# The ELU of a half step's last tile behind the next half step's copy, two places for g and tanh, and weight sums and conversions at other hooks

## The chip, the core and the metric

One core of a Trainium2 chip runs the kernel. The metric is the device time of one launch in microseconds. The core has TensorE (PE, matrix products), VectorE (DVE), ScalarE (ACT), GpSimd (POOL) and SyncE (SP, which here only issues DMAs). Each engine takes its instructions in the order of its own queue, and a wait in front of an instruction holds all that stand behind it in that queue.

## What is computed

Three layers follow one another: a linear attention whose q and k go through a softmax, a mixture of four experts on its output, and a feed-forward layer with ELU. Inputs of the last layer's weights come as float64.

```python
def reference(q, k, v, domain_probs, w1, w2, w_in, w_out):
    q_s = softmax(q over head_dim); k_s = softmax(k over seq)
    kv = einsum('bhsd,bhse->bhde', k_s, v)
    x = einsum('bhsd,bhde->bhse', q_s, kv) -> (2304, 512)
    p = domain_probs / sum(domain_probs)
    x = sum over e of p[:, e] * (relu(x @ w1[e]) @ w2[e])   # w1 (4,512,1024)
    h = x @ w_in                                            # (512, 2048)
    return where(h > 0, h, exp(min(h, 0)) - 1) @ w_out      # (2048, 512)
```

## The kernel before

**Precision and products.** Every float32 operand of a matmul is split into a high part and a low part, and a product takes three matmuls (high by high, high by low, low by high). The first product of a block (tokens by hidden columns) is made from seven partial products of quarter blocks instead of eight, with sums and differences of quarters of the weights and of the tokens.

**Steps.** The first part of the run does the attention, and the first expert unit plainly beside it. From about 290 us on the work goes in 30 steps, numbered i, which are pairs (s, b): s = 0 to 9 is a group of hidden columns, b = 0 to 2 a third of the 2304 tokens. s = 0 to 5 belong to the experts (s below 5 in a form with a fast second product, `second_product`), s = 6 to 9, from about 842 us, to the ELU layer. A change of s comes every three steps.

**Half steps.** A step has two half steps, and each of them seven products p0 to p6 of six 128x384 matmuls (L1110), which go into four PSUM banks A, B, C, D; in the second half step A changes its part with C, and B with D. Behind p1, p3 and p5 stands a chunk each: twelve 128x512 matmuls (L1162 to L1164) of the second product of the step before. What the other engines do behind each product:

- p0: ACT copies C_ to a tile s5 (L1307).
- p1: ACT copies B_ to A_ (L1309). p2 writes into B_ again, so p2 waits for this copy.
- p2: DVE adds D_ = B_ + s5 (L1312). p4 writes into B_ again.
- p3: A_ is finished: ELU of A_.
- p4: DVE adds C_ = B_ + s5 (L1319).
- p5: D_ is finished: ELU of D_, and behind the chunk ELU of C_.
- p6: B_ is finished: ELU of B_, the half step's last tile, in the code right ahead of the next half step's p0.

**ELU of a tile** (`elu`): relu, exp and tanh on ACT (L1134 to L1136; m, e_ and t), e_ = (e_ + 1) t on DVE (L1137), then `flush()`, which issues the parts of the tile before (high part gh on ACT, L1144; low part gl on POOL, L1145), then g = max(h, 0) + e_ on DVE (L1140). The parts of g wait in a list until the next tile's flush. t and g have one place each (tags qh and ql), so a tile's g can be written only when the parts of the tile before have been made. e_ has one place too; it and s5 are two halves of one buffer, which the rows show as `extra`. In the rows a tile is named by the bank or the buffer it uses: m and h are PSUM banks or m tiles, and xh, xl, hpa and gx are buffers that take parts.

**What sets the order.** Side work is laid on numbered hooks: `at(t, fn)` in the attention part, `at2(i, k, fn)` in the steps, SH = 24 hooks in each step. A hook runs when PE's program reaches it, so a hook's number sets where in the queues of DVE, ACT, POOL and SP its instructions stand. `w1_steps` makes the high and low parts of four weight tiles for one s and half: hi(k) on ACT (L734), lo(k) on DVE (L744), and the differences `sums1` and `sums2` on DVE (L748 to L754); its dictionary gives the hook of each, with 13 more for the first half's, which stand in the last step of the s before. `convert` turns a 128x512 tile of float64 weights into float32: five DVE instructions (L455, L461, L465, L471, L474), an exp on ACT (L468) and a store in ACT's queue (L477); its load is issued on SP some hooks earlier. There are 32 such conversions. The evacuations of the second product are on DVE too (L1271 in the fast form, L1169 and L1175 in the chunks), those of s = 6 on ACT (L1173).

Of the kernel before, what the change touches and what calls it, by code (L numbers as in the profile page):

```python
# [21 lines left out]
def tile_attention_moe_moe(  # L22
# [692 lines left out]
    def w1_steps(s, p):  # L715

        r, t = [], []

        def begin():
            r.append(w1r.pop((s, p)).rearrange("p j (d f) -> p j d f", d=KD))  # L720
            for _ in range(4):
                t.append(wp.tile([P, 2, KD, P], F32R, tag="w1", name="w1s"))
            if s % 2:
                t[0], t[2] = t[2], t[0]
            hi(0)

        def src(k):
            return (r[0][:, 0], r[0][:, 1, 2:], r[0][:, 1], r[0][:, 0])[k]

        def dst(k, hl):  # L730
            return t[k][:, hl, :2] if k == 1 else t[k][:, hl]

        def hi(k):
            nc.scalar.activation(out=dst(k, 0), in_=src(k), func=AF.Copy)  # L734
            if k == 3:
                w1s[s, p] = dict(
                    A11=(t[0], 0), A12=(t[0], 2), A22=(t[1], 0),
                    S1=(t[2], 0), S2=(t[2], 2), S3=(t[3], 0), S4=(t[3], 2),
                )

        tt = nc.vector.tensor_tensor

        def lo(k):
            tt(out=dst(k, 1), in0=src(k), in1=dst(k, 0).bitcast(F32), op=ALU.subtract)  # L744

        def sums1():
            f1, f2 = r[0][:, 0], r[0][:, 1]
            tt(out=f1[:, :2], in0=f1[:, :2], in1=f2[:, :2], op=ALU.subtract)  # L748
            tt(out=f2[:, :2], in0=f2[:, :2], in1=f2[:, 2:], op=ALU.add)

        def sums2():
            f1, f2 = r[0][:, 0], r[0][:, 1]
            tt(out=f2[:, 2:], in0=f2[:, 2:], in1=f1[:, :2], op=ALU.subtract)
            tt(out=f1[:, 2:], in0=f1[:, 2:], in1=f2[:, 2:], op=ALU.subtract)  # L754

        m = int(s >= S_MOE)
        return {
            -5: begin, -4: lambda: lo(0), -2: sums1, 0: lambda: hi(1), 1: lambda: lo(1), 4: sums2,
            6 - m: lambda: hi(2), 7 - m: lambda: lo(2), 9 - m: lambda: hi(3), 11 - 2 * m: lambda: lo(3),
        }  # L760

    w2g = {}
# [68 lines left out]
    NCONV = 2 * F2 // P  # L831
    later = lambda n, fn: at2(0, n, fn)
    end1 = NB * S_FAST * SH
    CONV = [(at, t, 2, True) for t in (12, 30, 48, 122, 142, 160)]
    CONV += [(later, 34 + 26 * n, 3, False) for n in range(13)]
    CONV += [(later, end1 + 13 + 14 * n, 1, True) for n in range(3)]
    end2 = NB * S_MOE * SH
    CONV += [(later, end2 + 2 + 14 * n, 1, True) for n in range(NCONV - len(CONV))]
    for s, (put, t, d, aside) in enumerate(CONV):
        put(t - 8, lambda s=s, x=aside: convert_load(s, x))  # L840
        for n, fn in zip((0, 1, 2, 3, 5, 6, 8), convert(s, aside)):
            put(t + d * n, fn)
    for i, (s, b) in enumerate(STEPS):
        more = s + 1 < len(STEPS) // NB
        if b == 0:
# [7 lines left out]
        if b == 0:  # L853
# [11 lines left out]
            if s == S_MOE:  # L865
                a1, b1, a2, c2, b2, d2 = (42, 42, 72, 77, 82, 91)
            elif s == S_MOE + 1:
                a2, b2, c2, d2, a1, b1 = (21, 23, 29, 33, 38, 42)
            elif s == S_MOE + 2:
                a2, b2 = (14, 16)  # L870
            if s >= S_FAST:
                at2(i, a2, lambda s=s: w_load(s + 1, 0, 1))
                at2(i, b2, lambda s=s: w_load(s + 1, 1, 1))
# [246 lines left out]
            out=gl, in0=h, scalar=0.0, in1=gh.bitcast(F32), op0=ALU.max, op1=ALU.subtract  # L1120
        )

    waiting = []

    def flush():
        while waiting:
# [2 lines left out]
    def elu(i, h, f, half):  # L1129


        m = tmp.tile([P, TB], F32, tag="y", name="m")
        t = tmp.tile([P, TB], F32, tag="qh", name="t")
        nc.scalar.activation(out=m, in_=h, func=AF.Relu, scale=-1.0)  # L1134
        nc.scalar.activation(out=e_, in_=m, func=AF.Exp, scale=-1.0)  # L1135
        nc.scalar.activation(out=t, in_=m, func=AF.Tanh, scale=-0.5)  # L1136
        nc.vector.scalar_tensor_tensor(out=e_, in0=e_, scalar=1.0, in1=t, op0=ALU.add, op1=ALU.mult)  # L1137
        flush()
        g = tmp.tile([P, TB], F32, tag="ql", name="g")
        nc.vector.scalar_tensor_tensor(out=g, in0=h, scalar=0.0, in1=e_, op0=ALU.max, op1=ALU.add)  # L1140
        gh, gl = take(i, half, f)

        def parts():
            nc.scalar.activation(out=gh, in_=g, func=AF.Copy)  # L1144
            nc.gpsimd.tensor_tensor(out=gl, in0=g, in1=gh.bitcast(F32), op=ALU.subtract)  # L1145

        waiting.append(parts)
# [142 lines left out]
    for i, (s, b) in enumerate(STEPS):  # L1290
# [5 lines left out]
        for fp in range(2):  # L1296
# [5 lines left out]
            for p in range(len(PRODUCTS)):  # L1302
# [5 lines left out]
                elif p == 1:  # L1308
                    nc.scalar.activation(out=A_, in_=B_, func=AF.Copy)  # L1309
                    flush_late()  # L1310
                elif p == 2:
                    nc.vector.tensor_tensor(out=D_, in0=B_, in1=s5, op=ALU.add)  # L1312
                elif p == 3:
# [13 lines left out]
                elif p == 6:  # L1327
                    if idx in PLACES and fast(i - 1):
                        second_product(i - 1, PLACES.index(idx))
                    if fast(i):  # L1330
                        last = quarter_a12(i, fp, B_)
                        flush_late()
                        late.append(last)
                    else:
                        act(i, B_, f2, 0)
                if fp == 1:
                    if p == 0:
                        ring_load(len(OPS) * (i + 1))
# [10 lines left out]
                if p == 5 and not fast(i):  # L1349
                    if moe:  # L1350
                        relu(i, D_, f1, 1)
                    act(i, C_, f2, 1)
    flush()
    for c in CHUNKS:
        queue.append((len(STEPS) - 1, c))
# [54 lines left out]
```

## Time and profile before

| | before |
|---|---|
| median of 3 runs | 1293.41 us (1289.06 to 1294.11) |
| the profiled execution, its own time | 1294.12 us |
| its span in the profile | 1292.3 us |
| PE, matmul | 1209.5 us busy (94%) |
| PE, weight loads | 1110.5 us (86%) |
| DVE | 840.0 us (65%) |
| ACT | 631.8 us (49%) |
| POOL | 509.5 us (39%) |
| granted TensorE clock, mean | 0.98 of 2.4 GHz |

Busy shares are means over the run. An engine's idle time matters where another waits for it, so the views that count are the waits (per engine, which instruction waited, for whom, how long) and the timeline of single stretches. A row of the timeline may stand for several equal instructions (x2); the idle time and its releaser in brackets are those ahead of the first. Ends of matmuls are modelled: a 128x384 matmul reads 0.33 us, while the next one starts 0.17 us later.

### The profile page before, as it was taken

Reading aid. Unit: us, or ns where it says so; the run is one execution under the profiler, and the core shown is the slowest. Engines: PE = TensorE matmul, PEld = TensorE weight load, DVE = VectorE, ACT = ScalarE, POOL = GpSimd, SP = SyncE. Lnnn points to the kernel's source line nnn. Section 1 sums busy time; section 2 is a strip of 40 time slices with the busy share of each in tenths; the row PEclk is TensorE's granted clock in tenths of the full one; section 3 lists DMA queues with packets and bytes.
Section 4 is the critical chain, followed back from the end, with each engine's and each line's share of the span. In section 5 each row is a group of like instructions: output and inputs, shape, how many; then the busy total and the mean of one; then the engine's idle time right before and its main releaser. Section 6 shows DMA issues by size and latency. Waiting matters only on the chain.

```text
span 1292.3 us, 20568 instructions
## 1 busy us (share of the span) xinstructions
PE 1209.5 (94%) x7336; PEld 1110.5 (86%) x7336; DVE 840.0 (65%) x1486; ACT 631.8 (49%) x1361; POOL 509.5 (39%) x484
## 2 busy tenths in 40 slices
PE   7799999999999999999999999988888999999998
PEld 6588888888999999999999998877777878888887
DVE  6877787545676686776777765667465565456443
ACT  6444543235445454445554434546566445555442
POOL 4522552007446456455456423237223322322221
PEclk7899998999999999999999999999999999999999
DMA  8454565816656657657667578988757554644442
GB/s 223 138 150 147 191 206 209 284 57 225 241 195 241 230 181 268 225 190 268 224 214 257 191 281 267 336 276 273 285 187 269 177 204 170 215 166 154 167 165 82
DMA packets 155174, 272.32 MB, mean 211 GB/s; under 512 B 12864, under 2 KB 77888, under 8 KB 155072
## 3 DMA queue, kind: packets, MB, share of 16 engines
q1 hardware_dynamic: 145856, 254.23, 58.1%
q10 hardware_dynamic: 9216, 16.78, 3.5%
q8 instruction: 58, 0.95, 0.3%
q14 instruction: 44, 0.36, 0.1%
HBM read 224.83 MB, written 46.14 MB: 210 GB/s over the span
## 4 chain that ended last, share of the span: by engine, by line
PE 57%; DVE 18%; ACT 10%; issue 5%; POOL 5%; DMA 4%; SPq 0%; ACTq 0%; DVEq 0%; POOLq 0%
PE o L1249 14%; PE m L1110 11%; PE h L1110 10%; PE o L974 6%; PE h L974 6%; DVE g L1140 2%; ACT t L1136 2%; PE o L1164 2%; PE o L1163 2%; PE o L1162 2%; DVE accB L1271 1%; ACT extra L1135 1%; DVE w1s L744 1%; DMA r<-in_w_dram 1%; POOL xh L1145 1%
## 5 line engine op out<-in xcount | busy, mean ns | idle before, releaser
L1110 PE MATMUL m<-xh,w1s 128*128 128x384 f32 x840 | 251.1, 344 | 40.7 <-ACT h L1309 16.5
L1110 PE MATMUL h<-xh,w1s 128*128 128x384 f32 x840 | 247.0, 340 | 13.8 <-ACT m L1309 13.0
L1110 PEld LDWEIGHTS m<-xh,w1s 128*128 128x128 f32 x840 | 156.5, 191 | 53.1 <-ACT h L1309 21.1
L1110 PEld LDWEIGHTS h<-xh,w1s 128*128 128x128 f32 x840 | 156.1, 190 | 21.5 <-ACT m L1309 18.5
L1110 PE MATMUL m<-xl,w1s 128*128 128x384 f32 x420 | 142.6, 340 | 0.0
L1110 PE MATMUL h<-xl,w1s 128*128 128x384 f32 x420 | 141.8, 338 | 0.0
L1137 DVE SCALAR_TENSOR_TENSOR extra<-extra,t 128x384 f32<-128x384 f32 x96 | 58.5, 610 | 101.3 <-ACT t L1136 101.1
L974 PE MATMUL o<-w2t,hpa 128*128 128x512 f32 x432 | 120.2, 406 | 1.2 <-DVE hpa L1006 1.0
L974 PE MATMUL h<-xh,w1t 128*128 128x256 f32 (+1 forms) x512 | 114.1, 301 | 0.1
L974 PEld LDWEIGHTS h<-xh,w1t 128*128 128x128 f32 x512 | 88.0, 196 | 5.3 <-POOL w1t L421 0.4
L1249 PE MATMUL o<-w2g,xh 128*128 128x256 f32 x540 | 91.5, 284 | 0.0
L974 PEld LDWEIGHTS o<-w2t,hpa 128*128 128x128 f32 x432 | 77.0, 192 | 15.5 <-DVE hpa L1006 2.8
L1249 PE MATMUL o<-w2g,hpa 128*128 128x256 f32 x540 | 88.9, 282 | 0.0
L1249 PE MATMUL o<-w2g,xl 128*128 128x256 f32 x540 | 87.6, 283 | 0.0
L1135 ACT ACTIVATE extra<-m 128x384 f32<-128x384 f32 x96 | 50.4, 525 | 64.9 <-DVE g L1140 63.1
L1110 PEld LDWEIGHTS m<-xl,w1s 128*128 128x128 f32 x420 | 80.1, 191 | 1.2
L1110 PEld LDWEIGHTS h<-xl,w1s 128*128 128x128 f32 x420 | 79.8, 190 | 1.2
L1249 PEld LDWEIGHTS o<-w2g,xh 128*128 128x128 f32 x540 | 79.4, 193 | 0.0
L974 PE MATMUL h<-xl,w1t 128*128 128x256 f32 (+1 forms) x256 | 78.5, 307 | 0.0
L1249 PEld LDWEIGHTS o<-w2g,hpa 128*128 128x128 f32 x540 | 76.2, 190 | 0.0
L1249 PEld LDWEIGHTS o<-w2g,xl 128*128 128x128 f32 x540 | 76.1, 191 | 0.0
L775 POOL TENSOR_TENSOR w2g<-r,w2g 128x512 fp32r<-128x512 f32 x35 | 47.3, 1363 | 57.2 <-ACT w2g L774 57.2
(263 smaller groups left out, 2873.6 us busy)
## 6 DMA issues: line engine op xcount, KB each, us to landing
xh<-xs SPq DMA_DIRECT2D x210, 384.0 KB, 5.3
xl<-xs SPq DMA_DIRECT2D x210, 384.0 KB, 6.0
r<-in_w_dram SPq DMA_DIRECT2D x60, 256.0 KB, 4.0
xs<-stage SPq DMA_DIRECT2D x43, 256.0 KB, 3.6
xs<-xh SPq DMA_DIRECT2D x21, 384.0 KB, 4.4
xs<-xl SPq DMA_DIRECT2D x21, 384.0 KB, 4.3
r<-scratch ACTq DMA_DIRECT2D x28, 256.0 KB, 5.9
gt<-in_w_out_dram SPq DMA_DIRECT2D x10, 512.0 KB, 5.3
```

Source lines behind the costliest of these rows:

```text
L744: tt(out=dst(k, 1), in0=src(k), in1=dst(k, 0).bitcast(F32), op=ALU.subtract)
L775: nc.gpsimd.tensor_tensor(out=t[:, 1], in0=src, in1=t[:, 0].bitcast(F32), op=ALU.subtract)
L974: nc.tensor.matmul(out, lhsT, rhs, **kw)
L1110: nc.tensor.matmul(dst, t[:, wl, c + dl, :], x[xl_][:, dl, :], start=(n == 0 and p < 2), stop=(n == 5), skip_group_check=True,)
L1135: nc.scalar.activation(out=e_, in_=m, func=AF.Exp, scale=-1.0)
L1136: nc.scalar.activation(out=t, in_=m, func=AF.Tanh, scale=-0.5)
L1137: nc.vector.scalar_tensor_tensor(out=e_, in0=e_, scalar=1.0, in1=t, op0=ALU.add, op1=ALU.mult)
L1140: nc.vector.scalar_tensor_tensor(out=g, in0=h, scalar=0.0, in1=e_, op0=ALU.max, op1=ALU.add)
L1162: nc.tensor.matmul(o, gh, w[:, 0, :], start=(f == 0), stop=False)
L1163: nc.tensor.matmul(o, gh, w[:, 1, :], start=False, stop=False)
L1164: nc.tensor.matmul(o, gl, w[:, 0, :], start=False, stop=(f == FS - 1))
L1249: nc.tensor.matmul(o, l, r, start=(first_write and m == 0 and c != 1), stop=(m == 5), skip_group_check=True)
```

## The change

Five things are done. First, the ELU of B_ behind p6 is put in a list, `later_elu`, and taken from it behind the next half step's A_ copy (L1309 of before). Second, t and g get two places each, used in turn (`halves`). Third, in `w1_steps` the second high part goes from hook 0 to -1, its low part from 1 to 0, `sums2` from 4 to 1, the third high part from 6 (5 in the ELU layer) to 4, its low part from 7 (6) to 5, the fourth high part from 9 (8) to 8, and its low part from 11 (9) to 10 (9). Fourth, the conversions: in the attention part five instead of six, none of them at 122; in the fast steps 15 at a distance of 22 hooks instead of 13 at 26, and within one the pieces stand closer together; then three at 12 hooks' distance instead of 14; in the ELU steps nine instead of ten, the first 40 hooks into that layer instead of 2, so that step 18 has none. Fifth, one weight load (b2 for s = 8) moves from hook 16 to 18.

```diff
@@ w1_steps
-            -5: begin, -4: lambda: lo(0), -2: sums1, 0: lambda: hi(1), 1: lambda: lo(1), 4: sums2,
-            6 - m: lambda: hi(2), 7 - m: lambda: lo(2), 9 - m: lambda: hi(3), 11 - 2 * m: lambda: lo(3),
+            -5: begin, -4: lambda: lo(0), -2: sums1, -1: lambda: hi(1), 0: lambda: lo(1), 1: sums2,
+            4: lambda: hi(2), 5: lambda: lo(2), 8: lambda: hi(3), 10 - m: lambda: lo(3),
@@ conversions
-    CONV = [(at, t, 2, True) for t in (12, 30, 48, 122, 142, 160)]
-    CONV += [(later, 34 + 26 * n, 3, False) for n in range(13)]
-    CONV += [(later, end1 + 13 + 14 * n, 1, True) for n in range(3)]
+    CONV = [(at, t, 2, True) for t in (12, 30, 48, 146, 164)]
+    CONV += [(later, 34 + 22 * n, 2, False) for n in range(15)]
+    CONV += [(later, end1 + 13 + 12 * n, 1, True) for n in range(3)]
...
-    CONV += [(later, end2 + 2 + 14 * n, 1, True) for n in range(NCONV - len(CONV))]
+    CONV += [(later, end2 + 40 + 12 * n, 1, True) for n in range(NCONV - len(CONV))]
...
-        put(t - 8, lambda s=s, x=aside: convert_load(s, x))
-        for n, fn in zip((0, 1, 2, 3, 5, 6, 8), convert(s, aside)):
-            put(t + d * n, fn)
+        put(t - 7, lambda s=s, x=aside: convert_load(s, x))
+        for n, fn in zip((0, 1, 2, 3, 4, 5, 7) if d == 1 else (0, 2, 4, 6, 10, 12, 16), convert(s, aside)):
+            put(t + n, fn)
@@ elu
-        t = tmp.tile([P, TB], F32, tag="qh", name="t")
+        if not halves:
+            for tag in ("qh", "ql"):
+                halves[tag] = tmp.tile([P, 2 * TB], F32, tag=tag, name="half")
+        k = slice(turns[0] % 2 * TB, (turns[0] % 2 + 1) * TB)
+        turns[0] += 1
+        t, g = halves["qh"][:, k], halves["ql"][:, k]
...
-        g = tmp.tile([P, TB], F32, tag="ql", name="g")
@@ steps, behind p1
                     nc.scalar.activation(out=A_, in_=B_, func=AF.Copy)
                     flush_late()
+                    while later_elu:
+                        elu(*later_elu.pop(0))
@@ steps, behind p6
-                    else:
-                        act(i, B_, f2, 0)
+                    elif moe:
+                        relu(i, B_, f2, 0)
+                    else:
+                        later_elu.append((i, B_, f2, 0))
```

**ACT at a boundary of two half steps near the end.** L1307 and L1309 are the two copies of the new half step (L1312 and L1314 of after), the trio L1134 to L1136 (L1140 to L1142) is the ELU of a tile, L1144 (L1149) the high part. Before:

```order
L1134 ACTIVATE m_12065<-m_2883 128x384
L1135 ACTIVATE extra_2884<-m_12065 128x384
L1136 ACTIVATE t_12066<-m_12065 128x384
L1144 ACTIVATE xl_91<-g_12048 128x384
L1134 ACTIVATE m_12081<-m_2882 128x384
L1135 ACTIVATE extra_2884<-m_12081 128x384
L1136 ACTIVATE t_12082<-m_12081 128x384
L1144 ACTIVATE xh_90<-g_12073 128x384
L1307 ACTIVATE extra_2884<-h_2880 128x384
L1309 ACTIVATE m_2883<-h_2881 128x384
```

After:

```order
L1140 ACTIVATE m_11891<-m_2875 128x384
L1141 ACTIVATE extra_2876<-m_11891 128x384
L1142 ACTIVATE half_8692<-m_11891 128x384
L1149 ACTIVATE xl_91<-half_8693 128x384
L1312 ACTIVATE extra_2876<-h_2872 128x384
L1314 ACTIVATE m_2875<-h_2873 128x384
L1140 ACTIVATE m_11919<-m_2874 128x384
L1141 ACTIVATE extra_2876<-m_11919 128x384
L1142 ACTIVATE half_8692<-m_11919 128x384
L1149 ACTIVATE xh_90<-half_8693 128x384
```

The trio of the last tile and the high part that it flushes have moved from ahead of the two copies to behind them.

**DVE at a change of s in the fast steps.** L1271 (L1276 of after) are evacuations of the second product, L744 the low parts of the weights; `w1s_4492` is the one of the third tile that the next step's products read, L753 and L754 are `sums2`. Before:

```order
L455 TENSOR_SCALAR ce_97<-x64_4547 128x512
L1319 TENSOR_TENSOR h_2880<-h_2881,extra_2884 128x384
L1201 SCALAR_TENSOR_TENSOR xl_91<-h_2880,xl_91 128x384
L1206 SCALAR_TENSOR_TENSOR gt_96<-m_2882,gt_96 128x384 x2
L1215 TENSOR_TENSOR gt_96<-gt_96 128x384
L1271 SCALAR_TENSOR_TENSOR accB_93<-o_3110,pn_86,accB_93 128x256 x3
L744 TENSOR_TENSOR w1s_4492<-r_4232,w1s_4492 128x512
L744 TENSOR_TENSOR w1s_4655<-r_4279,w1s_4655 128x512
```

After (there the tile is `w1s_4493`):

```order
L753 TENSOR_TENSOR r_4230<-r_4230 128x256
L754 TENSOR_TENSOR r_4230<-r_4230 128x256
L1319 TENSOR_TENSOR m_2874<-h_2873,extra_2876 128x384
L1276 SCALAR_TENSOR_TENSOR accB_93<-o_3102,pn_86,accB_93 128x256 x3
L744 TENSOR_TENSOR w1s_4493<-r_4230,w1s_4493 128x512
L1326 TENSOR_TENSOR h_2872<-h_2873,extra_2876 128x384
L1206 SCALAR_TENSOR_TENSOR xl_91<-h_2872,xl_91 128x384
L1211 SCALAR_TENSOR_TENSOR gt_96<-m_2874,gt_96 128x384 x2
```

The low part now stands ahead of the C_ add (L1319, L1326 of after) and of what follows that add, one group of evacuations earlier; the next tile's L744 is no longer its neighbour.

**DVE in the attention part, at hook 122.** L1006 makes a part of the first expert unit, L238 and L240 are the sums that the attention's ek is made from.

```order
 L322 TENSOR_REDUCE qm<-accB 96x12
 L647 TENSOR_TENSOR sum<-sum,xl 128x2x384
-L455 TENSOR_SCALAR ce<-gt 128x512
 L1006 SCALAR_TENSOR_TENSOR hpa<-h,hpa 128x256
 L238 TENSOR_TENSOR ek<-m,ek 128x512
 L240 TENSOR_TENSOR ek<-m,ek 64x128
-L461 TENSOR_SCALAR gt<-gt 128x512
 L388 TENSOR_TENSOR xl<-m,xh 128x576
```

The conversion's first two instructions no longer stand there.

## Rows read from the trace of the kernel before

**Rows 1.** Waits of PE, 842 us to the end: total us, times, longest us.

```profile
PE m L1110 <- ACT h L1309: 14.9, 10, 4.1
PE h L1110 <- ACT m L1309: 12.6, 12, 2.4
PE m L1110 <- DVE m L1319: 5.0, 3, 2.9
PE m L1110 <- DVE g L1140: 1.6, 1, 1.6
PE o L1164 <- POOL xh L1145: 1.3, 2, 1.0
```

**Rows 2.** Waits of PE, 290 to 842 us.

```profile
PE m L1110 <- DVE w1s L744: 13.0, 5, 3.1
```

**Rows 3.** Waits of DVE, 842 us to the end.

```profile
DVE g L1140 <- POOL xh L1145: 23.8, 23, 2.4
```

**Rows 4.** Timeline of a half step: start, us, engine, line, operation [idle before, releaser].

```profile
1235.53 0.56 DVE L1140 SCALAR_TENSOR_TENSOR g<-m,extra 128x384 f32<-128x384 f32 x1 [0.95 <-POOL gx L1145]
1238.01 0.33 PE L1110 MATMUL m<-xh,w1s 128*128 128x384 f32 x1
1238.18 0.39 PE L1162 MATMUL o<-w2s,xh 128*128 128x512 f32 x1
...
1238.67 0.56 DVE L1140 SCALAR_TENSOR_TENSOR g<-h,extra 128x384 f32<-128x384 f32 x1 [0.95 <-POOL hpa L1145]
...
1240.95 0.48 ACT L1309 ACTIVATE h<-m 128x384 f32<-128x384 f32 x1
1241.48 0.44 PE L1110 MATMUL m<-xh,w1s 128*128 128x384 f32 x1 [0.38 <-ACT h L1309]
...
1242.89 0.57 DVE L1312 TENSOR_TENSOR h<-m,extra 128x384 f32<-128x384 f32 x1
...
1243.67 0.39 PE L1162 MATMUL o<-w2s,xh 128*128 128x512 f32 x1
...
1246.43 0.33 PE L1110 MATMUL m<-xh,w1s 128*128 128x384 f32 x1
```

**Rows 5.** Windows: us, busy PE, PEld, DVE, ACT, POOL, clock, DMA share, GB/s.

```profile
193.00:201.00 8.00, 5.46 (x32) 4.64 (x33) 6.72 (x16) 4.44 (x9) 2.22 (x2) 0.65 0.27 101
553.00:561.00 8.00, 8.00 (x46) 8.00 (x47) 6.75 (x12) 2.52 (x5) 1.86 (x2) 0.79 0.44 139
927.00:935.00 8.00, 7.81 (x40) 7.17 (x41) 4.00 (x7) 3.59 (x8) 1.47 (x2) 1.00 0.57 196
1000.00:1008.00 8.00, 6.43 (x19) 5.90 (x20) 2.24 (x4) 4.12 (x10) 1.17 (x2) 0.57 0.00 1
```

**Rows 6.** Timeline around the longest wait on L1309: ACT and PE.

```profile
995.29 0.60 ACT L1173 ACTIVATE accB<-o 128x512 f32<-128x512 f32 x1 [4.57 <-PE m L1110]
...
1001.57 0.69 PE L1110 MATMUL m<-xh,w1s 128*128 128x384 f32 x1 [4.12 <-ACT h L1309]
```

**Rows 7.** Timeline at the first change of s: DVE and PE.

```profile
364.21 2.10 DVE L744 TENSOR_TENSOR w1s<-r,w1s 128x512 fp32r<-128x512 f32 x2
...
364.94 0.62 PE L1110 MATMUL m<-xh,w1s 128*128 128x384 f32 x2 [2.33 <-DVE w1s L744]
```

**Rows 8.** Timeline in the attention part: DVE and PE.

```profile
190.44 3.45 DVE L455 TENSOR_SCALAR ce<-gt 128x512 uint16<-128x512 uint16 x1
...
195.54 0.70 PE L283 MATMUL m<-accB,ek 128*64 128x65 f32 x8 [3.46 <-ACT ek L244]
```

**Rows 9.** Timeline of DVE in step 18.

```profile
856.35 1.21 DVE L471 SCALAR_TENSOR_TENSOR ce<-gt,ce 128x512 uint16<-128x512 uint16 x1
```

**Rows 10.** Instructions of L1137 and L1140: ns minimum/median/maximum, first and last start.

```profile
L1137 DVE SCALAR_TENSOR_TENSOR extra<-extra,t x96: 541/559/1370, 850.6 to 1272.8; 128x384 f32<-128x384 f32 x96
...
L1140 DVE SCALAR_TENSOR_TENSOR g<-h,extra x48: 556/558/560, 851.7 to 1274.3; 128x384 f32<-128x384 f32 x48
```

More of the change, by code (lines that the diff above doesn't have):

```diff
@@ L869, in tile_attention_moe_moe @@
             elif s == S_MOE + 2:
-                a2, b2 = (14, 16)
+                a2, b2 = (14, 18)
             if s >= S_FAST:
@@ L1121, in relu @@
         )
-    waiting = []
+    waiting, later_elu = [], []
+    halves, turns = {}, [0]
     def flush():
@@ L1352, in tile_attention_moe_moe @@
                     act(i, C_, f2, 1)
+    while later_elu:
+        elu(*later_elu.pop(0))
     flush()
```

## The prediction, made before the change was run

> **What bounds the kernel now.** TensorE (PE) is busy nearly all the time, so a change that leaves its instructions and their order alone can only shorten the stretches in which it stands still or runs at half its clock. I read PE's waits by stage first. In the ELU stage (842 us to the end) two rows tell most of it: PE waits for ACT's copy A_<-B_ (L1309) for 14.9 and 12.6 us, over 22 of the 24 half steps [rows 1]. In the stage before, PE waits five times, 13.0 us in all, for DVE's weight parts (L744), once at each change of s [rows 2]. Then I asked what makes the copy late, with DVE's waits: g (L1140) waits for POOL's gl (L1145), 23.8 us in the largest of four such rows, one for each buffer that gl writes [rows 3]. The timeline of an undisturbed half step shows the chain [rows 4]: g(D) starts only when POOL is done (0.95 idle), C's tile follows, g(C) waits 0.95 again, the last tile B's ACT work follows that, and the copy of the next half step comes last, at 1240.95. PE was through with its chunk 0.38 before 1241.48, when it starts p2. p1, whose result the copy reads, was over at 1238.01 + 0.33 = 1238.34. So the copy was ready to run 2.6 us before it did.
>
> The third loss is the granted clock. It is at the upper level, 2.4 GHz, in most of the run, and in a few stretches PE drops to 1.2 GHz for a part of them, each time just behind a long wait: 8 us stretches at a mean of 0.65, 0.79 and 0.57 [rows 5]. Four read 0.79 (at 553, 865, 960 and 1056 us; one stands in the rows) and one 0.82 (at 361 us). One minus the mean, times 8, is what each lost at most: 2.8 + 4 x 1.7 + 1.4 + 3.4 = 14.4 us.
>
> **The change part by part. The last tile's ELU behind the copy, and two places for t and g.** These belong to one chain. Work it out on [rows 4]. g(D) at 1235.53 had stood 0.95 behind a free DVE. With a second place it needs no POOL and starts about 1234.6. exp(C) waits for g(D) alone, and one tile later g(C) runs at about 1236.8 to 1237.4 rather than 1238.67. B's relu, exp and tanh no longer stand ahead of the copy. The s5 copy goes when p0 is over, and the A copy when p1 is: 1238.34 plus its 0.48 is 1238.87, against 1241.43. It is 2.56 us earlier, and 2.2 us before PE runs dry (1241.48 - 0.38), so in the steady half step the wait goes wholly. Where a half step is disturbed, 2.56 us are there to take it up. The longest wait is 4.12 us [rows 6], and the nine others of its row come to 14.9 - 4.1 = 10.8, 1.2 each; so 4.12 - 2.56 = 1.6 us stay. That one comes from ACT's queue: its 4.57 idle before 995.29 lies behind a conversion's store (L477), which waits for DVE. Gain: 27.5 - 1.6 = 25.9 us. The first matmul behind a wait also takes 0.44 against 0.33 [rows 4]; 27 waits (22 here, 5 below) x 0.11 are 2.9 us more.
>
> What this adds: the parts of C now run behind the copy and behind B's relu, exp and tanh. Chunks read them, but from step 20 on none before p3's, which starts at 1243.67 [rows 4], and by the chain above they are done near 1241.8. In step 19 the first chunk reads them at once, and its wait on POOL (1.3 us in two [rows 1]) changes place rather than going: nothing taken, 1.3 either way. g(B) and e_(B) now stand ahead of the D_ add (L1312) in DVE's queue. The add ended at 1243.46, and p4, which overwrites what it reads, starts at 1246.43 [rows 4], so there are 3.0 us of room; g(B), by the chain above, is done near 1241.5, before the add ran in the old order. Nothing taken; the third rival prices the other case. At the end of the kernel the last ELUs stand in their old order: nothing.
>
> **Weight sums and parts at earlier hooks.** The wait at 364.94 shows the chain: two L744 of 1.05 each, started at 364.21, behind the evacuations of the second product, and PE waits 2.33 [rows 7]. In the new order the second L744 comes later, and the one that PE needs (lo2) stands one hook earlier. The last evacuation ahead of it is released by a matmul 38 before the need, not 8. Thirty matmuls of 384 columns at 0.17 apart (1238.01 to 1238.18 [rows 4]) are 5.1 us; with 256 columns, two thirds of that, 3.4. The longest of the five waits is 3.1 [rows 2]. All 13.0 go; the other end is 5 x (3.1 - 2.3) = 4 us that stay, if a stretched DVE instruction of a microsecond gets between.
>
> **Conversions at other hooks.** In the attention stage DVE's L455 at 190.44 took 3.45 us, and 3.46 us of PE's wait for ek follow it through L1006, L238 and ACT [rows 8]. In the new order no L455 stands there: -3.2, between 0 (some other long row in its place) and -3.46. In step 18 conversions are gone; L471 at 856.35 took 1.21 [rows 9] just ahead of the C_ add (L1319) for which PE waited 2.9 of the 5.0 us [rows 1]. Taken: -2.9, and -1.6 for the one wait on g (L1140), a bank that now frees a POOL wait sooner; between 0 and -6 together. What comes in their place: two conversions more in the stage before 842 us, at 22 hooks' spacing instead of 26, and two in each of the steps 20 to 23. Each is five DVE instructions; of the two whose rows stand here one took 1.21 and one 3.45 us [rows 8, 9]. Nearly all of it lies beside PE's work; for the pieces that come out I take +5, about two such conversions, between 0 and +18 (first rival).
>
> **Clock.** If the waits go, the lapses behind them should go too, but not every long wait had one (behind a wait at 927 us the clock read 1.00 [rows 5]), so the tie is loose, and smaller waits stay. I take two thirds of 14.4: -9.6, between 0 and -14.4.
>
> **Sum.** -25.9 - 2.9 - 13.0 - 3.2 - 4.5 + 5 - 9.6 = -54.1 us. The profiled run took 1294.12 for a span of 1292.3, 0.7 above the median of 1293.41, so 1240.0 stands against that run and the median alike. Everything at its best gives -25.9 - 1.6 - 2.9 - 13.0 - 3.46 - 6 - 14.4, or -67: 1227.
>
> **Rivals.** *First: half of it arrives.* The conversion's store sits in ACT's queue and holds ACT until DVE is through: 4.57 us at 995.29 [rows 6]. Conversions in the ELU stage now follow each other at 12 hooks, not 14. If each of the nine there costs ACT as much, 2.0 us over the room of 2.56 come out on PE: 18 us. With such waits the lapses of the clock stay, 9.6: 1240 + 27.6, about 1268. Against it: ten conversions ran in that stage, and the waits on L1309 show one of 4.1 us and the rest at 1.2 on average [rows 1].
>
> *Second: DVE and POOL get in each other's way.* So far g waits for POOL, so the two take turns. Freed of it, e_ (L1137) can run beside gl. Its median is 0.559 and its longest 1.370 us [rows 10]. Two on the path in a half step, 0.81 longer each, are 1.6 x 24 = 39 us: 1279. Against it: by the chain above gl(D) is issued behind C's tanh, so it runs beside g(C), not beside e_, and g, with one operand in PSUM, stayed within 556 to 560 ns in the 48 cases of one form [rows 10], and the other form reads alike. The Trainium skill (GPSIMD Engine Reference, section 1, Specifications) states that GpSimd shares its SBUF interfaces with VectorE and contends with instructions that have two SBUF inputs. By that rule e_ would be the one to pay, and the time would be this rival's; the spread of e_ agrees with the rule, the constancy of g too.
>
> *Third: slower.* g(B) ahead of the D_ add makes p4 late. The add has 3.0 us of room. It would take a whole L455 of 3.45, an L471 of 1.21 and an e_ stretched by 0.81 ahead of it in the queue [rows 8 to 10]: 5.5 us, 2.5 over the room. In all 24 half steps that is 60 us, and the clock's 9.6 stay: 1310. Against the gain of 54 it decides from 54 / 24 = 2.3 us over the room in each half step, fewer where the lapses stay. Against it: only nine conversions are left for the stage.
>
> *Fourth: nothing moves.* PE's waits are only passed on to the next thing that is late, a load or a weight part, and the clock stays as it is: 1290. Against it: no load stands among PE's long waits [rows 1], and the steady half step shows no other wait than the 0.38.
>
> **How the numbers follow.** Chances: forecast 0.63, first rival 0.20, second 0.05, third 0.05, fourth 0.07. The predicted time is 1240. The range goes from 1224, a little below the best sum, to 1272, which takes in the first rival with its spread and leaves out the others. A measurement of this kernel tells about 0.5%, 6.5 us, from no change. Faster by more: 0.63 + 0.20 + 0.05 = 0.88; within it 0.07; slower 0.05.
>
> **What would show it.** In the new trace: PE's waits on the A copy in the ELU stage under 4 us in all; no wait of g on POOL in a steady half step; the copy ending near p1's end plus 0.5; no wait for L744 over 0.5 us at the five changes of s; no L455 of 3 us before ek; the granted clock at 1.00 in most of the seven stretches. The forecast is wrong if the copies still wait for POOL or for the store, if the D_ add or the C_ add becomes what PE waits for, if e_ has a median well over 0.56, or if the clock's lapses stay although the waits are gone.

## The result

The changed kernel took 1238.42 us (median of 3 runs, 1238.21 to 1239.69), the kernel before 1293.41: a ratio of 0.959, 95% interval 0.955 to 0.962. The forecast was 1240.0, in a range of 1224 to 1272. The profiled run of after took 1239.69 for a span of 1237.9 us; that of before 1294.12.

The page of after begins like this (busy us of each engine, share of the span, instructions):

```profile
span 1237.9 us, 20542 instructions
...
PE 1194.2 (96%) x7336; PEld 1101.8 (89%) x7336; DVE 846.2 (68%) x1486; ACT 635.4 (51%) x1361; POOL 511.3 (41%) x484
```

PE has the same 7336 matmuls in a shorter span; DVE's and ACT's busy time is what it was to 1%. Work was not saved, it was put elsewhere. Where the 54.4 us of span went is seen by three marks that both kernels have: the first s5 copy (the start of the steps), the first relu of the ELU (the start of the ELU stage), and the end.

| stage | before | after | difference |
|---|---|---|---|
| to the first s5 copy | 279.5 us | 273.0 us | -6.5 |
| steps of s = 0 to 5, to the first ELU | 569.1 | 559.3 | -9.8 |
| ELU stage | 443.7 | 405.6 | -38.1 |

PE's waits in the ELU stage of after, largest first (total us, times, longest), answer to [rows 1]. L1314 is the old L1309 (the A copy), L1326 the old L1319 (the C_ add), L1319 the old L1312 (the D_ add):

```profile
PE m L1110 <- ACT h L1314: 5.6, 4, 2.5
PE h L1110 <- ACT m L1314: 2.5, 2, 1.7
PE m L1110 <- DVE m L1326: 0.9, 2, 0.5
PE m L1110 <- DVE h L1319: 0.6, 1, 0.6
```

The copy costs 8.1 us in six half steps, not 27.5 in 22. In the steps before (283 to 826 us, to be read beside [rows 2]) the wait on the weights' low parts is gone, and another stands in its place, the D_ add, 8.4 us instead of 1.4:

```profile
PE h L1110 <- DVE m L1319: 4.5, 4, 1.5
PE m L1110 <- DVE h L1319: 3.9, 6, 1.2
PE m L1110 <- ACT h L1314: 1.6, 2, 1.4
```

In DVE's waits in the ELU stage g has no row on POOL any more; [rows 3] and its three like have vanished. (One small row on POOL is left there, 3.3 us, of a weight's staging tile.) What DVE waits for most is tanh:

```profile
DVE extra L1143 <- ACT half L1142: 126.1, 78, 4.4
```

A steady half step of after answers to [rows 4] (start, us, engine, line). The first row is g(D), the third g(C); then the two copies, p1's last matmul, the chunk's last and p2's first:

```profile
1182.10 0.56 DVE L1145 SCALAR_TENSOR_TENSOR half<-m,extra 128x384 f32<-128x384 f32 x1
...
1183.72 0.56 DVE L1143 SCALAR_TENSOR_TENSOR extra<-extra,half 128x384 f32<-128x384 f32 x1 [0.38 <-ACT half L1142]
1184.38 0.56 DVE L1145 SCALAR_TENSOR_TENSOR half<-h,extra 128x384 f32<-128x384 f32 x1
...
1184.75 0.49 ACT L1312 ACTIVATE extra<-m 128x384 f32<-128x384 f32 x1 [0.65 <-PE m L1110]
1185.79 0.47 ACT L1314 ACTIVATE h<-m 128x384 f32<-128x384 f32 x1 [0.55 <-PE m L1110]
...
1185.42 0.33 PE L1110 MATMUL m<-xh,w1s 128*128 128x384 f32 x1
...
1188.13 0.39 PE L1169 MATMUL o<-w2s,hpa 128*128 128x512 f32 x1
1188.36 0.33 PE L1110 MATMUL m<-xh,w1s 128*128 128x384 f32 x1
```

Both copies now wait for PE, not PE for them: the A copy starts when p1 ends (1185.42 + 0.33) and is done at 1186.26, 2.1 us before p2 starts at 1188.36 with no idle time. The prediction had worked out 2.2 us.

The granted clock reads 1.00 in the windows of after where the lapses of [rows 5], the stretches at the lower level, would lie; three of them (columns as there):

```profile
192.00:200.00 8.00, 8.00 (x67) 7.12 (x67) 6.91 (x14) 3.78 (x9) 2.91 (x2) 1.00 0.39 146
...
544.00:552.00 8.00, 6.93 (x51) 6.61 (x50) 6.94 (x11) 4.37 (x9) 2.67 (x2) 1.00 0.49 145
...
960.00:968.00 8.00, 5.50 (x28) 4.64 (x27) 2.00 (x4) 5.41 (x12) 1.53 (x2) 1.00 0.68 230
```

### The profile page after: what moved, and what is told of

The parts are those of the page before. It is cut to its first block, busy times and chain, and to the rows that moved or that the text cites. A ratio compares the mean times of both kernels' runs of the same rounds, so it can differ in the third digit from the quotient of the medians.

```text
span 1237.9 us, 20542 instructions
## 1 busy us (share of the span) xinstructions
PE 1194.2 (96%) x7336; PEld 1101.8 (89%) x7336; DVE 846.2 (68%) x1486; ACT 635.4 (51%) x1361; POOL 511.3 (41%) x484
## 4 chain that ended last, share of the span: by engine, by line
PE 72%; DVE 15%; ACT 5%; DMA 4%; issue 3%; POOL 0%; ACTq 0%; SPq 0%; DVEq 0%; POOLq 0%
PE o L1254 14%; PE h L1110 13%; PE m L1110 13%; PE h L974 7%; PE o L974 7%; PE o L1169 5%; PE o L1168 5%; PE o L1167 5%; DVE accB L1276 1%; DVE w1s L744 1%; DMA xl<-xs 1%; PE m L375 1%; DMA xs<-stage 1%; DVE ce L471 1%; DVE r L783 1%
## 5 line engine op out<-in xcount | busy, mean ns | idle before, releaser
L1110 PE MATMUL m<-xh,w1s 128*128 128x384 f32 x840 | 246.5, 339 | 14.8 <-ACT h L1314 7.2
L1143 DVE SCALAR_TENSOR_TENSOR extra<-extra,half 128x384 f32<-128x384 f32 x96 | 57.5, 599 | 126.1 <-ACT half L1142 126.1
L974 PEld LDWEIGHTS o<-w2t,hpa 128*128 128x128 f32 x432 | 76.0, 190 | 15.3 <-DVE hpa L1006 2.9
L744 DVE TENSOR_TENSOR w1s<-r,w1s 128x512 fp32r<-128x512 f32 x80 | 68.3, 859 | 4.0 <-ACT w1s L734 4.0
```

Of the source, the lines that this page charges most:

```text
L974: nc.tensor.matmul(out, lhsT, rhs, **kw)
L1110: nc.tensor.matmul(dst, t[:, wl, c + dl, :], x[xl_][:, dl, :], start=(n == 0 and p < 2), stop=(n == 5), skip_group_check=True,)
```

## The experiments

Twelve runs, in three groups. The fifth part of the change, the weight load two hooks later, stands in none of the runs on the kernel before and was not tried by itself. It belongs to step 24. From the A copy just ahead of that step (the twelfth of the ELU stage) to the end a_elu without it takes 222.9 us and after with it 223.8, so no gain of it can be seen. A stage time below is taken by the same three marks. "Clock lost" is the sum, over 8 us windows from 48 us on that read under 0.97, of 8 times one minus the granted clock; the last window, which the end of the run cuts off, is left out. (Ahead of 48 us PE is at the lower level for a part of the time in either kernel: the granted clock averages 0.83 there in before and 0.75 in after.) By that count before lost 17.3 us, 15.3 of them behind 190 us (the prediction had counted 14.4 in its windows), and the profiled run of after none.

### One part undone on the changed kernel

**u_defer**: the last tile's ELU back ahead of the copy.

```diff
-                    elif moe:
-                        relu(i, B_, f2, 0)
-                    else:
-                        later_elu.append((i, B_, f2, 0))
+                    else:
+                        act(i, B_, f2, 0)
```

> The changed kernel with one part undone: the ELU of the last tile stands ahead of the next half step's copy again; two places for t and g stay, and all hooks as changed. Theory: the two places alone already bring the copy ahead of the chunk's end in a steady half step. With g(C) done near 1237.4 on the clock of the old steady half step, exp and tanh of B, the high part of C and the two copies follow at once and end near 1239.7, against PE running dry at 1241.1; 1.4 us of room are left instead of 2.2. So only the disturbed half steps pay, some 1 us each: 1238.4 + 4 to 8, about 1244, PE's waits on the A copy 10 to 16 us instead of 8. Rival: the deferral does the work, since ACT's queue is what the copy waits for; then nearly the whole 20 us of PE's waits on the copy come back: 1256 to 1262.

Measured: 1259.38 us, ratio to before 0.975 (0.972 to 0.978): +21 on after, the rival's number. ELU stage 424.9 us against 405.6, the other stages as in after. The waits of its ELU stage:

```profile
PE m L1110 <- ACT h L1314: 12.9, 6, 4.3
PE h L1110 <- ACT m L1314: 9.1, 6, 2.5
```

The theory is right for the steady half steps and wrong in size for the rest. Behind 1060 us, where no conversions run any more, only one half step waits for the copy (0.56 us); but all ten from 882 to 1050 us, the stretch of the conversions, do, with 0.8 to 4.3 us each. That is 22.0 us instead of 8.1, and the clock lost up to 6.8 us on top, which the theory had left out: 13.9 + 6.8 = 20.7, about the 19.3 of the stage.

**u_two**: one place each for t and g.

```diff
-        if not halves:
...
-        t, g = halves["qh"][:, k], halves["ql"][:, k]
+        t = tmp.tile([P, TB], F32, tag="qh", name="t")
...
         flush()
+        g = tmp.tile([P, TB], F32, tag="ql", name="g")
```

> The changed kernel with one part undone: one place each for t and g, the deferral and all hooks as changed. Theory: g waits for POOL again in every tile (some 80 us of DVE idle in all), but the copy stands ahead of B's relu, exp and tanh. It has to wait only for g(C), which reads the bank that the copy writes: near 1239.2 on the clock of the old steady half step, so the copy ends near 1239.8, 1.3 us before PE runs dry. Only disturbed half steps pay: 1238.4 + 4 to 8, about 1244. Rival: the two places do the work, and without them the copy is late in every half step by the old 0.4 to 2 us: 1256 to 1262. A third outcome, the deferred tile making the D_ add late when g(B) waits for POOL as well, would show as waits on the D_ add (L1319 of the changed kernel) in the ELU stage, over 5 us.

Measured: 1266.59 us (1262.13 to 1269.34), ratio 0.980 (0.977 to 0.983): +28, the rival's side and above even its range. In its profile (its fastest run; this kernel's line numbers from the copy on are four less than those of after) the copy costs 18.5 us in ten half steps, and the waits of g on POOL are back. Two of their four rows, and the two on the copy:

```profile
PE m L1110 <- ACT h L1310: 10.6, 6, 3.5
PE h L1110 <- ACT m L1310: 7.9, 4, 2.5
...
DVE g L1141 <- POOL xh L1146: 25.8, 26, 1.6
DVE g L1141 <- POOL xl L1146: 24.4, 26, 1.0
```

What ACT waits for names the reason: the copy (L1310) waits for g(C) 34.9 us in all, since g(C) reads the bank that the copy is to write.

```profile
ACT h L1310 <- DVE g L1141: 19.0, 11, 3.6
...
ACT m L1310 <- DVE g L1141: 15.9, 11, 1.9
```

The third outcome did not come: the D_ add costs 1.5 us. Again the steady half steps, behind 1060 us, do not wait for the copy, but for one that waits 0.18 us. So either ELU part is enough where nothing disturbs, and both are needed where a conversion runs.

**u_w1**: the dictionary of `w1_steps` as before.

> The changed kernel with the weight sums and parts at their old hooks. Theory A: the waits on the low weight parts come back, 13 us in five, with up to 3 us of clock; but the D_ add, for which PE waits 8.4 us between 283 and 826 us in the changed kernel, is late there because the second weight sums now stand ahead of it in DVE's queue, so those 8 go: net +5 to +8, 1244 to 1246. Theory B: the D_ add is late because the conversions are denser; then the 8 stay and the net is +13 to +16, 1252 to 1254.

Measured: 1253.06 us, ratio 0.969 (0.967 to 0.972): +14.6. Steps before the ELU 573.5 us, 14.2 more than after; ELU stage 405.8, unchanged. Its waits from 275 to 830 us:

```profile
PE m L1110 <- DVE w1s L744: 15.5, 5, 4.4
PE h L1110 <- DVE m L1319: 1.9, 3, 0.9
```

In mechanism it is theory A: 6.5 of the 8.4 us on the D_ add go, so the D_ add was late because of the weight sums. In time it is theory B's number, because the low parts cost 15.5 instead of 13 and up to 8.5 us of clock were lost in that stage, where I had put 3. The waits, 15.5 - 6.5 = 9.0, and the clock, at most 8.5, more than cover the 14.2.

**u_conv**: the conversions as before.

> The changed kernel with the conversions at their old hooks. The attention part loses 3.5 us for ek's wait and up to 2.8 us of clock, step 18 about 2.9 us on the C_ add. Theory A (the D_ add's 8 us between 283 and 826 us belong to the weight sums): these stay, and the time is +7 to +11, about 1247. Theory B (they belong to the denser conversions): they go, and the time is +0 to +3, about 1240.

Measured: 1243.88 us, ratio 0.963 (0.960 to 0.965): +5.5, between the two, but the trace decides: the D_ add still costs 8.2 us before the ELU (4.9 and 3.3), so theory A holds. The 3.5 us on ek are back, and 2.6 on the C_ add in step 18. The time fell short of theory A because the ELU stage got no worse (405.1 us against 405.6): there the old conversions, 14 hooks apart, leave the copy waiting 1.3 us only, not 8.1.

### One part alone on the kernel before

**a_elu**: deferral and two places alone.

> The kernel before with the two ELU parts alone (deferral and two places), all hooks as before. If the parts of the change add up, this brings what the ELU stage gained but for step 18: PE's waits on the copy from 27.5 to 1 to 8 us, 6.8 of the 8.5 us of clock there, first matmuls 2.4: -28 to -35, 1258 to 1265. PE's waits on the copy: near 1 us if conversions at 14 hooks' distance leave the copy alone, as the run with the old conversions showed (1.3), near 8 if not. Rival: the ELU parts need the other hooks to work, and the time stays over 1270.

Measured: 1259.38 us, ratio 0.974 (0.972 to 0.976): -33, as expected in time. ELU stage 411.5 us. Its waits from 830 us on show what the ELU parts do not touch, the C_ add of step 18 and the next one:

```profile
PE m L1110 <- DVE m L1326: 5.8, 2, 2.9
...
PE m L1110 <- ACT h L1314: 0.7, 2, 0.3
PE h L1110 <- ACT m L1314: 0.6, 1, 0.6
```

The clock did not come back as expected: this profiled launch lost 8.6 us of it in the ELU stage, as much as before, though the copy is waited for 1.3 us only. Two of its stretches at the lower level, in the windows at 856 (0.57) and 960 us (0.64), stand at the two waits of 2.9 us on the C_ add. The copy's 26.2 us and the first matmuls behind 19 waits fewer (0.11 each) make 28.3 of the stage's 32.2 us; the rest was not traced.

**a_hooks**: weight sums and conversions alone.

> The kernel before with the hooks alone (weight sums and conversions as changed), the ELU in its old order with one place each. The attention part gains 6.3 us (3.5 of wait, 2.8 of clock), the steps up to 842 us about 10, step 18 about 2.9. In the ELU stage conversions stand closer together, and ELU's chain has no room: the waits on the copy stay at 27 us or grow by up to 6. Expected 1272 to 1279. The sum of this gain and that of the ELU parts alone should be near 54 us; a rival in which the parts need each other would leave the sum under 40.

Measured: 1293.30 us, ratio 1.0004 (0.9993 to 1.0016): no change, outside the expected 1272 to 1279. The stages say why: 273.2, 559.1 and 460.9 us. The first two gain 16.3 us, as much as in after; the ELU stage gives 17.2 back. Its waits on the copy (compare [rows 1]):

```profile
PE m L1110 <- ACT h L1309: 21.9, 10, 5.0
PE h L1110 <- ACT m L1309: 18.7, 12, 4.5
```

That is 40.6 us instead of 27.5, and 20.3 us of clock lost, all in this stage, instead of 8.5 there. A half step is 12 hooks long; with conversions 12 hooks apart each of the half steps from 905 to 1076 us meets one at the same place, and nine in a row wait 2.5 to 5.0 us. One of them, DVE and ACT (ACTq is ACT's queue issuing a DMA), then PE:

```profile
982.66 0.68 DVE L471 SCALAR_TENSOR_TENSOR ce<-gt,ce 128x512 uint16<-128x512 uint16 x1
983.38 0.69 DVE L474 SCALAR_TENSOR_TENSOR gt<-gt,ce 128x512 f32<-128x512 f32 x1
...
980.50 0.51 ACT L1144 ACTIVATE gx<-g 128x384 fp32r<-128x384 f32 x1
984.11 0.33 ACTq L477 DMA_DIRECT2D scratch<-gt  x1
984.53 1.33 ACTq L705 DMA_DIRECT2D r<-scratch  x2
985.91 0.60 ACT L1173 ACTIVATE accB<-o 128x512 f32<-128x512 f32 x1 [4.90 <-PE o L1164]
...
992.18 0.69 PE L1110 MATMUL m<-xh,w1s 128*128 128x384 f32 x1 [5.03 <-ACT h L1309]
```

ACT does nothing from 981.01 to 985.91. The row names PE as the releaser, but what stands ahead in ACT's queue is the store of the conversion (L477), issued right when DVE's L474 is done (984.07), and two loads behind it: 3.1 of the 4.9 us pass until the store can go, the rest goes to the three issues. The matmul that the row names, at 985.38, is the sixth of a chunk of twelve; the chunk that L1173 copies had ended by 981.3. The relu of the next tile, and with it the whole chain to the copy, starts after that.

So the two halves of the change do not add up when alone: -33.4 and +0.5 make -33, together they make -55. The new hooks are bad for the old ELU order and good for the new one.

### What is left: the store, the distance, the sums

**b_store**: the store of the conversions from s = 5 on three hooks later, on the changed kernel.

```diff
-        for n, fn in zip((0, 1, 2, 3, 4, 5, 7) if d == 1 else (0, 2, 4, 6, 10, 12, 16), convert(s, aside)):
+        for n, fn in zip((0, 1, 2, 3, 4, 5, 10) if d == 1 else (0, 2, 4, 6, 10, 12, 16), convert(s, aside)):
```

> The changed kernel with the conversion's store in the ELU stage (and the three ahead of it) three hooks later than now. Theory: the six waits on the copy that are left, 8.1 us, come from the store standing in ACT's queue until DVE's last conversion instruction is done; three hooks later it waits for nothing, the waits fall under 3 us and the time by 4 to 6: 1233. Rival: the waits come from g(C), which stands behind the conversion's instructions in DVE's own queue and which the copy must wait for; then they stay at 6 to 9 us and the time at 1238.

Measured: 1234.08 us (1233.94 to 1235.81), ratio 0.955 (0.954 to 0.956). The waits on the copy are 3.0 us instead of 8.1, ELU stage 401.5 us:

```profile
PE m L1110 <- ACT h L1314: 1.7, 2, 1.1
PE h L1110 <- ACT m L1314: 1.3, 3, 0.6
```

In the waits the theory holds. The times of this run and of after come from different chips, and the fastest launch of c_after below, 1235.13, lies within this run's range, so the 4.3 us between the medians are less sure than the waits. How a store makes the copy late is told by these rows of after, DVE and POOL, then ACT, then PE. They are the second longest of the six waits, 1.73 us; the longest, 2.50 us at 965.7, also has a store ahead of it (959.48) and two loads:

```profile
976.94 1.12 DVE L471 SCALAR_TENSOR_TENSOR ce<-gt,ce 128x512 uint16<-128x512 uint16 x1
978.09 1.66 DVE L474 SCALAR_TENSOR_TENSOR gt<-gt,ce 128x512 f32<-128x512 f32 x1
...
975.89 3.31 POOL L799 TENSOR_TENSOR w2s<-r,w2s 128x512 fp32r<-128x512 f32 x2
...
979.78 0.36 ACTq L477 DMA_DIRECT2D scratch<-gt  x1
980.18 0.49 ACT L1140 ACTIVATE m<-m 128x384 f32<-128x384 f32 x1 [4.29 <-DVE gt L474]
...
982.99 0.47 ACT L1314 ACTIVATE m<-h 128x384 f32<-128x384 f32 x1 [0.56 <-DVE half L1145]
...
983.52 0.44 PE L1110 MATMUL h<-xh,w1s 128*128 128x384 f32 x1 [1.73 <-ACT m L1314]
```

C's relu starts at 980.18, 4.29 us after ACT's last work, behind the store; then everything follows at its pace, and the copy is held 0.56 more by g(C). A part of the hold is DVE's: L471 and L474 took 2.78 us here beside POOL, 1.37 in the rows of a_hooks above.

**b_space**: nine conversions at 14 hooks' distance from hook 26 on, on the changed kernel.

> The changed kernel with the nine conversions of the ELU stage at 14 hooks' distance from hook 26 on, instead of 12 from hook 40 on; step 18 has still none. Theory: the distance is what disturbs the copy, and the waits on it fall from 8.1 to near the 1.3 us of the run with the old conversions, with nothing new in step 18: 1231 to 1233. Rival: it is the hooks on which the pieces fall, not the distance, and the waits only move: 1237 to 1240.

Measured: 1238.12 us, ratio 0.957 (0.956 to 0.959), no change in time: the rival. The copy's waits fall to 3.5 us, but the C_ add takes 3.2 (0.9 in after), and 3.9 us of clock were lost, 1.8 of them in the ELU stage.

**b_both**: b_store, and the second weight sums at hook 4 behind the D_ add, with the next parts at 5 and 6.

```diff
-            -5: begin, -4: lambda: lo(0), -2: sums1, -1: lambda: hi(1), 0: lambda: lo(1), 1: sums2,
-            4: lambda: hi(2), 5: lambda: lo(2), 8: lambda: hi(3), 10 - m: lambda: lo(3),
+            -5: begin, -4: lambda: lo(0), -2: sums1, -1: lambda: hi(1), 0: lambda: lo(1), 4: sums2,
+            5: lambda: hi(2), 6: lambda: lo(2), 8: lambda: hi(3), 10 - m: lambda: lo(3),
```

> The changed kernel with the conversion's store three hooks later and, besides, the second weight sums behind the D_ add again (hook 4, the third tile's high and low parts at 5 and 6). Theory: PE's waits on the D_ add in the fast steps, 9 us with the sums ahead of it, fall to 2 to 4, and the low parts at hook 6 are still early enough: 1234 - 5 to 7, 1227 to 1229. Rival: the low parts come late again, 1 to 3 us at each of the five changes of s: 1233 to 1245, with waits on L744 in the trace.

Measured: 1232.88 us (1231.87 to 1234.24), ratio 0.952 (0.950 to 0.954), the fastest here. In the steps before the ELU it did what was expected: 554.4 us against 559.3 in b_store, the D_ add at 2.7 us, no wait on L744 in the list:

```profile
PE m L1110 <- DVE h L1319: 2.5, 4, 1.2
PE m L1110 <- ACT h L1314: 2.0, 3, 1.4
```

The total missed the expected 1227 to 1229: the sums also stand later in the ELU stage, which took 405.5 us instead of 401.5, with 4.9 us on the copy and 2.5 on the C_ add. Whether the sums' hook or the 1.7 us of clock lost at 920 to 936 us is to blame was not separated. Against b_store, on another chip, the times lie 1.2 us apart and their ranges overlap.

**c_after**: the changed kernel again, on the chip of b_both.

> The changed kernel again, beside its variant with the later store on the same chip: 1238 to 1239. If it comes out within 1.5 us of the variant, the 4.3 us between them were the chip's.

Measured: 1239.38 us (1235.13 to 1241.63), ratio 0.957 (0.954 to 0.960). Launches of the same code differ in the clock: the profiled one here lost 3.2 us between 48 and 72 us, where that of after lost none, but ahead of 48 us its granted clock averages 0.85 against 0.75, so the clock alone does not explain the 1.9 us between the two. The median stands 6.5 us above b_both on the same chip, more than the 1.5 that would have put the difference down to the chip; how much of it is the store's and how much the sums' is not told by this pair.

**a_hooks_store**: the hooks alone on the kernel before, with the later store.

> The hooks alone on the kernel before, with the store of the conversions from s = 5 on three hooks later. With the hooks alone PE waited 40.6 us for the copy in the ELU stage and 20.3 us of clock were lost. Theory: the store that holds ACT's queue is what made every half step with a conversion late; without that hold the waits fall to 15 to 27 us, most of the lapses go with them, and the time to 1265 to 1278. Rival: the conversion's instructions in DVE's queue, ahead of e_ and g, make the chain late; then the waits stay over 35 us and the time over 1285.

Measured: 1273.35 us, ratio 0.984 (0.981 to 0.986): the same kernel as a_hooks but for three hooks of one DMA issue, and 20 us faster. ELU stage 439.5 us instead of 460.9, the clock lost 12.5 us in the run, 9.9 of them in that stage: about half of the loss came back, not most of it. The copy's waits:

```profile
PE h L1110 <- ACT m L1309: 13.6, 12, 2.5
PE m L1110 <- ACT h L1309: 13.3, 10, 3.3
```

That is 26.9 us, as in before. The store's place is shown to be the cause of what a_hooks gave back. The conversions are still 12 hooks apart here, so their distance is not enough to make the loss.

**a_store**: the later store alone on the kernel before.

> The kernel before with one thing changed: the store of the conversions from s = 5 on three hooks later. Of the 27.5 us of waits on the copy, ten half steps without a conversion make 0.4 each; the other 23 us belong to half steps with one. If the store is what makes these late, they fall by 10 to 18 us and some clock comes back: 1270 to 1282. If it is DVE's queue, 1289 to 1294.

Measured: 1284.54 us (1282.32 to 1291.31), ratio 0.993 (0.991 to 0.996): -9 to -10, less than the theory's range, though more than the rival's. The copy's waits fell from 27.5 to 22.0 us in the profiled launch, which is the slowest of the six and lost 21.0 us of clock. The longest wait, 4.1 us [rows 6], is 0.9 now, and one of 2.1 us at 867 is gone; the others moved by about 0.2 us at most. So in the old order most of what the copy waits for is not the store. That it is the chain itself, with the conversion's instructions in DVE's queue, fits but was not tried by itself.

## Why the prediction was right

Its total was 1.6 us off, which is in part luck: term by term it was less exact, and errors of opposite sign are hidden in the total. Two of its own signs of being wrong came up: the copy's waits are 8.1 us, not under 4, most of them behind the store, and the D_ add has become what PE waits for longest in the steps before the ELU.

- **The steady half step** was right in every link: g without POOL, the copy at p1's end, 2.1 us of room where 2.2 were worked out (1238.34 + 0.48 is 1238.82, not 1238.87; nothing hangs on it).
- **The waits on the copy** were to fall by 25.9 us and fell by 19.4. The step that was mis-sized is the room for disturbed half steps. It took the copy's start from p1's end alone; in a disturbed half step the copy also waits for g(C), which reads the bank that it writes (0.56 us in the row at 982.99), and the chain that starts late behind the store is as long as before from there on. The prediction let one wait out of the room, 1.6 us; there were six, 8.1 us. Its first rival had the right mechanism, the store in ACT's queue, and b_store and a_hooks_store show it.
- **The weights' low parts**: all 13.0 us went, as said (the text says that the needed part stands one hook earlier; it is two). What it did not see is that the sums ahead of it now stand in front of the D_ add: 8.4 us there, 1.4 before, shown by u_w1 and b_both. The +5 us that it had put in for the conversions covered most of it, for another reason.
- **The attention part**: -3.2 forecast for ek's wait, and the 3.5 us are gone; u_conv has them back. With the 2.8 us of clock that is -6.3, and the stage is 6.5 us shorter. So close a fit is partly chance: with the conversions at their old hooks the stage took 276.7 (a_elu), 277.5 (u_conv), 279.5 (before) and 280.5 us (a_store).
- **The other waits of the ELU stage**: -4.5 forecast; the C_ add went from 5.0 to 0.9, g's bank from 1.6 to 0.4: -5.3.
- **The clock**: two thirds of 14.4 taken, all of it came in the profiled run. By its own count this term was too small by 4.8 us. It is not the change's alone: c_after, the same code, lost 3.2 us near the start, and a_elu lost as much in the ELU stage as before with the copy's waits gone.
- **The second rival** (DVE and POOL in each other's way) did not come about. gl runs beside g now, in 85 of 96 tiles (overlaps of over 0.1 us; none before), and every g took 557 to 559 ns. e_ runs beside gl in 28 tiles (22 before), and has the same median as in [rows 10] and a smaller maximum. Thirteen of the 96 took over 0.6 us, each beside POOL (11 before), and all together lie 3.9 us over the median (4.9 before). By the Trainium skill's rule (GPSIMD Engine Reference, section 1, Specifications) instructions with two SBUF inputs, such as e_, contend with GpSimd. The trace agrees in these long e_ and in L474, with two SBUF inputs, which took 1.66 us beside POOL's two L799 (3.31 us), and 0.69 at 983.38 in a_hooks.

```profile
L1143 DVE SCALAR_TENSOR_TENSOR extra<-extra,half x96: 541/559/1128, 834.3 to 1217.3; 128x384 f32<-128x384 f32 x96
```

- **The third rival** (the D_ add late in the ELU stage) did not come about either: 0.6 us there in after.

Added up for the ELU stage: 19.4 + 5.3 of waits, 8.5 of clock, and about 0.7 each for two of step 19's waits make 34.6 of the 38.1 us. The first matmul behind each of some 16 waits fewer (0.11) gives 1.8 more; the last 1.7 us I did not trace.

What the prediction had wrong in kind, though not in number, is that it added the parts as if each had its price. a_elu and a_hooks show that in the ELU stage they have none by themselves. The new hooks are worth 15 to 16 us ahead of that stage in either kernel. In it they cost 17 us with the old ELU order (443.7 to 460.9) and gain 6 with the new one (411.5 in a_elu to 405.6 in after). Either half of the hooks alone brings those 6 us: 405.1 with the old conversions, 405.8 with the old sums. They arise ahead of the moved weight load: at the twelfth A copy, counted from the stage's start, a_elu is already 6.9 us behind after.

## What to carry to other kernels

Where a wait ends a chain, work out how much earlier the chain's end moves and compare it with when the engine that waits would run dry, in the steady case and with each kind of side work in it; the steady case here needed one of the two ELU edits, the disturbed ones both. A DMA issued from a compute engine's queue right behind the instruction that it waits for stops that engine as surely as arithmetic: try it some hooks later first; in the three kernels here that never cost time, and it brought from 4 to 20 us. Judge a schedule of side work with the loop's final order, not with the old one: the same hooks lost 17 us in one and gained 6 in the other. Side work at the loop's own length of 12 hooks met the same place in every half step; whether another distance helps was not shown (14 hooks with the new order changed no time).

## What the runs showed of the hardware

- The clock amplifies waits. By the count above, before lost 17.3 us to the lower level in its profiled run, a_hooks 20.3 and after none. In a_hooks the first matmul behind the waits of 4.16, 3.71, 5.03 and 4.46 us took 0.69 instead of 0.44, so PE was at 1.2 GHz when it went on; the granted clock of their windows (at 944, 968, 992 and 1016 us) is 0.79, 0.61, 0.62 and 0.84. The length of a wait does not tell by itself whether a lapse follows: in before one of 2.07 us at 867 had a lapse in its window (0.79), one of 2.66 at 927 had none ([rows 5], 1.00).
- The row that names the releaser of an ACT instruction does not name a DMA issue that stands ahead of it in the same queue: at 985.91 in a_hooks it names PE's L1164, whereas the 4.90 us of idle lie behind the store and two loads. The queue's own rows (ACTq) show it.
- A DVE instruction with a single input, on 16-bit words, was stretched eightfold beside POOL: L455 took 3.45 us at 190.44 [rows 8], and 0.41 at its shortest in the same run. POOL's rows of before there run from 189.79 to 193.61, all but the last 0.3 us of it. That POOL is the cause was not tried by itself.

```profile
189.79 2.06 POOL L328 TENSOR_TENSOR accB<-accB,qm 96x768 f32<-96x768 f32 x1 [5.78 <-issue]
191.82 1.79 POOL L653 TENSOR_TENSOR xl<-sum,xh 128x768 fp32r<-128x768 f32 x1
```
